# Turns of q, k, the landmarks and exp(C) by DMA from batch 3 and 2 on, scores over 64 rows, and a split first load

## The chip, the core and the metric

The kernel runs on one core of a Trainium2 chip. The core has five engines with their own instruction streams: PE (TensorE, matmuls; PEld is its weight load), DVE (VectorE), ACT (ScalarE), POOL (GpSimd) and SP (SyncE, which here only issues DMAs). PE writes to the accumulators (PSUM), the other engines read them from there; SBUF holds everything else. DMAs are issued from SP, ACT or POOL and run on 16 shared DMA engines. The metric is the device time of the program in microseconds; before the change it is 277.69 us, the median of three runs.

## What is computed

For 8 batches x 8 heads of 576 tokens with 64 features, a Nystrom attention with 32 landmarks, then a two-layer network with SiLU:

```python
q_lm = q.reshape(B, H, m, S // m, D).mean(axis=3)      # m = 32: means over 18 tokens
k_lm = k.reshape(B, H, m, S // m, D).mean(axis=3)
A  = sm(q, k_lm)        # 576 x 32 per head, sm: scaled softmax over the last axis
Bm = sm(q_lm, k_lm)     # 32 x 32
C  = sm(q_lm, k)        # 32 x 576
Z  = Bm^T / (norm_1(Bm) * norm_inf(Bm) + 1e-6)
for _ in range(6):
    Z = 2 * Z - Z @ Bm @ Z
attn = A @ Z @ C @ v
x = attn.transpose(0, 2, 1, 3).reshape(4608, 512)
h = x @ w_in            # 512 -> 2048
out = (h / (1 + exp(-h))) @ w_out                       # 2048 -> 512, float32
```

## The kernel before

**Tiling.** A batch is handled as a whole: its 8 heads are two halves (`qd` or `a`) of 4, and a head's 32 landmarks fill 32 partitions, so 4 heads x 32 landmarks make 128. q and k lie in SBUF as bf16 with partition = (head, landmark l) and in a row the 18 tokens of that landmark's segment (tiles `qn`, `kn`, two buffers each, one for even and one for odd batches).

**One batch's attention.** `landmarks` sums the 18 tokens of each segment: for batches 0 to 2 by PE with the identity as weights, from batch 3 on by a tree of additions on POOL (line 445, five for k and five for q). `turn` brings q and k into the form that PE needs, with the features on the partitions (tiles `qT`, `kT`, one buffer each): four DVE transposes of 128x576 words (lines 468 and 475); the landmarks are turned by one more (line 455, tile `lmT`). DVE turns 32x32 blocks of 4-byte words, so a word holds two features, and a score over 64 features becomes two matmuls over 32 rows (o = 0 and 1), accumulated. `scores_b`, `scores_a` and `scores_c` are those matmuls; from batch 2 on B and A go to PE as one group, C as another. A and C are written to the accumulators `h0` and `h1`. DVE transposes A's scores into `s_sb` (line 574) and takes maxima (lines 539, 590), POOL subtracts (596), ACT exponentiates: `pc` = exp(C) (line 620) and `ea` = exp(A) (line 631). `values` turns exp(C) with 12 matmuls against the identity (line 712) into `h0` and `h1`, copies it from there to `pt` (line 723: DVE; in batches 0 and 1 ACT copies one half), and multiplies by v (line 739). `steps_x` iterates Z with six small matmul and DVE steps (line 811), `z_of` closes it into `zt`.

**The network.** `mix` multiplies zt with w_in (4 heads x 2 halves, matmuls over 64 rows), through h0 and h1, into `m_sb`; `layer1` multiplies with A's weights `at` and applies SiLU (16 groups of four matmuls, alternately in h0 and h1, each with one ACT instruction of 576 columns, line 958) into `g`; `layer2` makes 128 tokens of output with 16 matmuls of 512 columns in one of two accumulators `o0`, `o1`, which ACT copies (line 989) into one of four `ost` buffers; SP issues the stores (line 1000). Two batches share a `g`, and layer 2 of a pair of batches has nine such tiles: the first four need only the even batch.

**What sets the order.** Nothing runs in program order. Every step is a node with an engine, a planned length, a priority, and the keys that it reads and writes; `_Plan.schedule` plays all engines against each other with those lengths, and the instructions are emitted in the planned order, each engine's in its own. On the chip each engine keeps that order and waits for semaphores. Steps that use the same buffer keep the order in which the program adds them: `SEQ` sets it (line 17: E is a batch's attention, S and X its first and second part, K its landmarks and turns, M the mix, L layer 1, after which the layer-2 tiles that are ready are added). `SHIFT` (line 21) moves the priorities of kinds of steps, `LOOK` is how far an engine may wait for a more urgent step, `dma_free` the planned time from which DMAs run. Layer 2 has the lowest priority on PE and fills it where nothing else is ready.

**Loads.** q, k and v of all batches and the weights are loaded by POOL, which turns float32 into bf16 on the way (lines 381, 382, 368); a load of k or q is two DMAs, one for each half of the partitions, so that heads lie in an order that `col` knows. Only batch 0's k comes from SP as float32 (`first_k`, lines 396 and 397), into space that `g` uses later, and is converted by DVE and ACT (lines 403 and 406). Batch b+2's loads are added behind batch b's attention.

Of the kernel before, what the change touches and what calls it, by code (L numbers as in the profile page):

```python
# [16 lines left out]
SEQ = ['E0', 'M0', 'S1', 'L0', 'X1', 'K2', 'M1', 'E2', 'L1', 'E3', 'M2', 'L2', 'M3', 'E4', 'L3', 'M4', 'E5', 'L4', 'E6', 'M5', 'L5', 'E7', 'M6', 'L6', 'M7', 'L7']  # L17
# [3 lines left out]
SHIFT = {'DVE gx t 3': 2.5, 'DVE qT qn 3': -0.25, 'DVE rn n 3': 0.5, 'POOL ea arec 1': 1, 'DVE amax s 3': -0.5, 'DVE lmT lm 3': 0.5, 'PE t gx 3': 2, 'DVE crec csum 3': -0.25, 'DVE asum ea 0': 2, 'POOL kn 1': -0.5, 'POOL s amax 2': 2, 'DVE s h 2': -0.5, 'DVE at ea 3': 2, 'DVE asum ea 2': 2, 'DVE kT kn 3': 1, 'ACT ea s 3': 0.5}  # L21

XM = 0.12

# [6 lines left out]
class _Plan:  # L31
# [3 lines left out]
    LOOK = 0.2  # L35
# [39 lines left out]
    def schedule(self):  # L75
# [4 lines left out]
        dma_free = 4.0  # L80
# [122 lines left out]
def kernel(  # L203
# [11 lines left out]
    LM = 32  # L215
# [32 lines left out]
    lm = [sb(f"lm{i}", [128, 2, 2, D], BF) for i in range(2)]  # L248
    lmT = [sb(f"lmT{i}", [128, 2, 2, LM, 2], BF) for i in range(2)]
# [5 lines left out]
    pc = sb("pc", [128, 2, 6, 96], BF)  # L255
# [53 lines left out]
    def emit_consts():  # L309
        V.memset(tiny, 0.0)  # L310
        V.memset(zero, 0.0)
        V.memset(mask, 0.0)
        V.memset(nmask, 0.0)
        V.memset(eps, 0.0)
        for a in range(4):
            V.memset(mask[32 * a:32 * a + 32, a, :], 1.0)
            V.memset(nmask[32 * a:32 * a + 32, a, :], -1.0)
            V.memset(eps[32 * a:32 * a + 1, :], 1e-6)
        V.memset(xp, 0.0)
        V.memset(heads_ps, 0.0)  # L320
        for a in range(4):
            V.memset(heads_ps[32 * a:32 * a + 32, a:a + 1], 1.0)
# [10 lines left out]
    def constants():  # L333
        P.add("DVE", 1.5, emit_consts, w=["mask", "xp", "zero", "tiny", "t0"], prio=-10)
# [29 lines left out]
    def load(t, src, b):  # L364
# [14 lines left out]
        def f():  # L379
            blk = rows.rearrange("(c p) n -> p c n", p=64)  # L380
            G.dma_start(out=dst[0:64], in_=blk[:, 0:4:3])
            G.dma_start(out=dst[64:128], in_=blk[:, 1:3])
        P.add("POOL", 1.4, f, w=nat_keys(t, 0) if b % 2 == 0 else [f"{t}n1"],
              dma=[1.4, 1.4], prio=-5 if b == 0 else -0.5)

    def first_k():


        st = g_sb[1].rearrange("p a n -> p (a n)").bitcast(FP)[
            :, 0:2 * SEG * D].rearrange("p (a i d) -> p a i d", a=2, d=D)  # L390
        rows = k[0].rearrange("h (l i) d -> (h l) (i d)", i=SEG).rearrange(
            "(c p) n -> p c n", p=64)
        flat = st.rearrange("p a i d -> p a (i d)")

        def f():
            nc.sync.dma_start(out=flat[0:64], in_=rows[:, 0:4:3])
            nc.sync.dma_start(out=flat[64:128], in_=rows[:, 1:3])
        P.add("SP", 1.25, f, w=["kst"], prio=-5, lat=4.0)
        for j, (i0, i1) in enumerate(((0, 7), (7, 12), (12, SEG))):
            src, dst = st[:, :, i0:i1], nat["k"][0][:, :, i0:i1]  # L400
            n = 2 * D * (i1 - i0)
            if j == 1:
                act(n, lambda src=src, dst=dst: A.copy(out=dst, in_=src),
                    r=["kst"], w=[f"kn0.{j}"], prio=-3)
            else:
                dve(n, lambda src=src, dst=dst: V.tensor_copy(out=dst, in_=src),
                    0.55, r=["kst"], w=[f"kn0.{j}"], prio=-3)
# [4 lines left out]
    def nat_keys(t, b):  # L412
        return [f"{t}n{b % 2}"] + [f"kn0.{j}" for j in range(3)] * (t == "k" and b == 0)

    def landmarks(b):
        p2 = b % 2
        for ti, t in ((1, "k"), (0, "q")):
            src = nat[t][p2]
            if b == 2:
# [3 lines left out]
            if b < 3:  # L423
                for i0 in range(0, SEG, 6):
                    def f(src=src, acc=acc, i0=i0):
# [4 lines left out]
                       w=[key], mode="full", prio=(0, 1.5, 0.5)[b], ni=12,  # L430
                       margin=0.8 * (b == 1))

                dst, src = lm[p2][:, ti], acc.rearrange("p (a d) -> p a d", d=D)
                if b == 1:
# [5 lines left out]
            else:  # L440
                tr, tk = tree, "tree"

                def add(o, a, c, n, r, w):
# [7 lines left out]
                add(lm[p2][:, ti], tr[:, :, 0], tr[:, :, 8], 128, [tk],  # L451
                    [f"lm{p2}.{ti}"])

# [9 lines left out]

    def turn(b):
        p2 = b % 2
        for qd in range(2):
# [6 lines left out]
        for qd in range(2):  # L473
# [5 lines left out]
            dve(576, f, r=[f"qn{p2}"], w=[f"qT.{qd}"], prio=3 if b else 0.9)  # L479
# [4 lines left out]
    def scores_b(b):  # L484
        lmr = lmT[b % 2]

# [12 lines left out]
        else:  # L499
            def both():  # L500
                f()
                for hf in range(2):
                    scores_a_of(b, hf)
            pe(0.6, both, r=[f"lmT{b % 2}", "qT.0", "qT.1"],
               w=["t0", "t1", "h0", "h1"], mode="32", prio=0.1, margin=0.2, ni=96)
# [16 lines left out]
    def scores_c(b):  # L522


        lmr = lmT[b % 2]
        def f():
# [9 lines left out]
        pe(0.53, f, r=[f"lmT{b % 2}", "kT.0", "kT.1"], w=["h0", "h1"], mode="32",  # L536
           prio=0.1, margin=0.2, ni=64)
# [22 lines left out]

    def scores_a(b):

        for hf, (i0, i1) in enumerate(HALF):
# [9 lines left out]
            if b > 1:  # L573
                dve(2 * n, lambda i0=i0, i1=i1, n=n, hf=hf: V.transpose(
                    out=s_sb[:, i0:i1].rearrange("p i a m -> p a i m"),
                    in_=h_ps[hf][:, :, 0:n].rearrange("p a (i m) -> p a i m", m=LM)), r=ks, w=[f"s{hf}"], prio=0.2)
# [29 lines left out]
    def exps_c(b):  # L606
# [12 lines left out]
        for qd in range(2):  # L619
            act(576, lambda qd=qd: A.activation(  # L620
                out=pc[:, qd].rearrange("p (j c) n -> p j (c n)", j=2),
                in_=h_ps[qd][:, :, 0:SH], func=AF.Exp, bias=cneg[:, qd:qd + 1],
# [4 lines left out]
    def exps_a(b):  # L627
        gate = gates(b)
        for hf, (i0, i1) in enumerate(HALF):
            n = 64 * (i1 - i0)  # L630
            act(1.3 * n, lambda i0=i0, i1=i1: A.activation(  # L631
# [493 lines left out]
```

## Time and profile before

| | us |
|---|---|
| time, three runs | 276.93, 277.69, 280.09 |
| the profiled execution: time, span from first to last instruction | 278.57, 276.9 |
| PE busy, DVE, ACT, POOL in the span | 252.8, 163.0, 165.3, 129.2 |
| layer-2 matmuls (592) busy | 142.4 |
| layer-1 matmuls (512) busy | 75.6 |
| ACT's SiLU (112 of 576 columns), mean | 0.651 |
| DVE turns of k and of q (16 each), median | 0.752, 0.755 |
| DVE copy of exp(C) turned, mean | 0.944 |
| POOL first addition of a landmark tree, mean | 2.37 |
| mean granted TensorE clock | 0.975 |

The page shows one execution. Busy times are a union over an engine's instructions; a matmul's end is modelled and overlaps the next one's start, so what a group of matmuls costs is read from starts. In a timeline each row has the start, the length, the engine, the line, the operation, output <- input, shape and how many instructions were merged; in brackets, how long the engine stood idle before it and what ended that. All matmuls have line 233, that of a helper; they are told apart by their tiles. The main groups in the page's list that touch the change:

```
L468 DVE STREAM_TRANSPOSE kT<-kn x16: 712/752/778, 13.6 to 191.3; 128x576 f32<-128x576 f32 x16
L723 DVE CAST pt<-h 96x768 bf16<-96x768 f32 x14 | 13.2, 944 | 0.0
L445 POOL TENSOR_TENSOR tree<-kn 128x1152 f32<-128x1152 bf16 x5 | 11.9, 2375 | 7.3 <-DMA kn<-in_k_dram
L596 POOL TENSOR_TENSOR s_sb<-s_sb,amax 128x512 f32<-128x512 f32 (+1 forms) x14 | 16.0, 1156 | 35.4 <-DVE amax L590
```

### The profile page before, as it was taken

How to read it: one execution, taken by the hardware profiler on the slowest of the kernel's cores; microseconds unless marked ns; L12 is line 12 of the kernel's file. 1: busy time of each engine (PE TensorE's matmuls, PEld its weight loads, DVE VectorE, ACT ScalarE, POOL GpSimd, SP SyncE). 2: the span in 40 equal slices, each digit the busy share in tenths (PEclk: the TensorE clock that was granted, in tenths of full speed). 3: DMA queues.
4: the chain of work that ended last, by engine and by line, in shares of the span. 5: the costliest groups of instructions: out<-in, count | busy, mean ns of one | idle time of the engine just before them, and what ended most of it. 6: DMA issues, size and time to landing. Idle time of an engine off the chain costs nothing.

```text
span 276.9 us, 6870 instructions
## 1 busy us (share of the span) xinstructions
PE 252.8 (91%) x2823; PEld 147.8 (53%) x2823; DVE 163.0 (59%) x388; ACT 165.3 (60%) x285; POOL 129.2 (47%) x155
## 2 busy tenths in 40 slices
PE   6178699889789999999999999999999999999994
PEld 4166475463466546645664467445755574664453
DVE  3178985997993995269936794798358822100000
ACT  2127768634686667837883688377827787761111
POOL 8234255869999999797729960321012300000000
PEclk9567999999999999999999999999999999999999
DMA  6999999999597139803593263112012210112334
GB/s 133 206 212 210 207 205 203 173 179 188 125 152 119 40 78 144 181 11 76 87 185 84 62 97 66 37 41 58 20 40 60 60 41 0 40 38 52 75 78 100
DMA packets 20288, 28.83 MB, mean 104 GB/s; under 512 B 2208, under 2 KB 11168, under 8 KB 20256
## 3 DMA queue, kind: packets, MB, share of 16 engines
q0 software_dynamic: 14048, 17.76, 39.1%
q1 hardware_dynamic: 6128, 10.56, 16.6%
q8 instruction: 22, 0.36, 0.6%
q10 hardware_dynamic: 80, 0.07, 0.1%
q14 instruction: 10, 0.08, 0.1%
HBM read 36.70 MB, written 9.44 MB: 167 GB/s over the span
## 4 chain that ended last, share of the span: by engine, by line
PE 72%; DVE 11%; DMA 6%; POOL 5%; ACT 2%; issue 2%; SPq 0%; POOLq 0%; DVEq 0%; ACTq 0%
PE o L233 39%; PE h L233 27%; PE t L233 6%; DMA g<-in_k_dram 4%; POOL tree L445 4%; DMA kn<-in_k_dram 3%; DVE pt L723 2%; DVE cmax L539 1%; DVE asum L898 1%; DVE crn L728 1%; POOL ea L907 1%; ACT g L941 1%; DVE amax L590 1%; ACT L958 0%; DVE s_sb L579 0%
## 5 line engine op out<-in xcount | busy, mean ns | idle before, releaser
L233 PE MATMUL o<-w_out_sb,g 128*128 128x512 bf16 (+1 forms) x592 | 142.4, 374 | 0.0
L233 PEld LDWEIGHTS <-g 128*128 128x128 bf16 x592 | 53.8, 98 | 52.1 <-issue 9.2
L233 PE MATMUL h<-at,m 128*128 128x288 bf16 (+2 forms) x512 | 75.6, 286 | 2.5 <-ACT m L886 1.3
L958 ACT ACTIVATE g<-h 128x576 bf16<-128x576 f32 x112 | 67.7, 651 | 14.2 <-PE h L233 14.2
L233 PEld LDWEIGHTS <-m 128*128 128x128 bf16 x512 | 49.2, 98 | 28.0 <-issue 3.8
L989 ACT COPY ost<-o 128x512 f32<-128x512 f32 (+1 forms) x37 | 21.2, 574 | 43.0 <-PE o L233 41.9
L596 POOL TENSOR_TENSOR s_sb<-s_sb,amax 128x512 f32<-128x512 f32 (+1 forms) x14 | 16.0, 1156 | 35.4 <-DVE amax L590 35.4
L840 DVE CAST m<-h 128x1024 bf16<-128x1024 f32 x14 | 17.0, 1214 | 15.7 <-PE h L233 15.7
L811 DVE SCALAR_TENSOR_TENSOR gx<-gx,t 128x384 bf16<-128x384 bf16 x30 | 16.3, 543 | 15.7 <-PE t L233 15.5
L445 POOL TENSOR_TENSOR tree<-tree 128x512 f32<-128x512 f32 (+2 forms) x30 | 24.7, 822 | 1.8
L907 POOL TENSOR_TENSOR ea<-ea,arec 128x640 bf16<-128x640 bf16 (+1 forms) x15 | 17.4, 1172 | 14.0 <-DVE arec L902 14.0
L843 ACT CAST m<-h 128x1024 bf16<-128x1024 f32 x14 | 14.2, 1012 | 14.5 <-PE h L233 14.5
L368 POOL DMA_DIRECT2D vn<-in_v_dram x24 | 14.2, 599 | 8.0 <-PE t L233 5.6
L620 ACT ACTIVATE pc<-h,cneg 128x576 bf16<-128x576 f32 x16 | 11.7, 734 | 6.5 <-DVE cneg L542 6.3
L445 POOL TENSOR_TENSOR tree<-kn 128x1152 f32<-128x1152 bf16 x5 | 11.9, 2375 | 7.3 <-DMA kn<-in_k_dram 7.2
L631 ACT ACTIVATE ea<-s_sb 128x512 bf16<-128x512 f32 (+1 forms) x16 | 13.1, 846 | 1.5 <-POOL s_sb L596 1.5
L723 DVE CAST pt<-h 96x768 bf16<-96x768 f32 x14 | 13.2, 944 | 0.0
L539 DVE TENSOR_REDUCE cmax<-h 128x1 f32<-128x576 f32 x16 | 11.4, 750 | 2.8 <-PE h L233 2.7
L233 PEld LDWEIGHTS <-ident 128*128 128x128 bf16 x108 | 8.3, 113 | 7.9 <-issue 7.8
L941 ACT ACTIVATE g<-h 128x512 bf16<-128x512 f32 (+1 forms) x16 | 9.6, 648 | 4.8 <-PE h L233 4.8
L445 POOL TENSOR_TENSOR tree<-qn 128x1152 f32<-128x1152 bf16 x5 | 11.9, 2371 | 0.4
L475 DVE STREAM_TRANSPOSE qT<-qn 128x576 f32<-128x576 f32 x16 | 11.9, 755 | 0.0
(123 smaller groups left out, 308.8 us busy)
## 6 DMA issues: line engine op xcount, KB each, us to landing
out_dram<-ost SPq DMA_DIRECT2D x70, 128.0 KB, 2.4
qn<-in_q_dram POOLq DMA_DIRECT2D x16, 288.0 KB, 8.2
vn<-in_v_dram POOLq DMA_DIRECT2D x24, 192.0 KB, 4.9
kn<-in_k_dram POOLq DMA_DIRECT2D x14, 288.0 KB, 8.4
w_out_sb<-in_moe_w_out_dram POOLq DMA_DIRECT2D x4, 512.0 KB, 16.2
w_in_sb<-in_moe_w_in_dram POOLq DMA_DIRECT2D x2, 768.0 KB, 15.8
g<-in_k_dram SPq DMA_DIRECT2D x2, 576.0 KB, 8.4
w_in_sb<-in_moe_w_in_dram POOLq DMA_DIRECT2D x2, 256.0 KB, 11.4
```

What stands on the lines that cost most here:

```text
L233: nc.tensor.matmul(out=out_ap, lhsT=lhsT, rhs=rhs, start=start, stop=stop, tile_position=tp, skip_group_check=True)
L368: G.dma_start(out=nat[t][b % 2][32 * t3:32 * t3 + 32].rearrange("p h j d -> p h (j d)"), in_=src[b].rearrange("h (l t j) d -> t l h (j d)" ...
L445: lambda: G.tensor_tensor(out=o, in0=a, in1=c, op=OP.add),
L539: dve(576, lambda qd=qd: V.tensor_reduce(out=cmax[:, qd:qd + 1], in_=h_ps[qd][:, :, 0:SH], axis=AX.XY, op=OP.max), r=[f"h{qd}"], w=[f"cmax ...
L596: E.tensor_tensor(out=sv, in0=sv, in1=mv.unsqueeze(2).to_broadcast((128, 2 * (i1 - i0), LM)), op=OP.subtract),
L723: dve(768, lambda dst=dst, src=src: V.tensor_copy(out=dst, in_=src), r=[f"h{qd}"], w=[f"pt{qd}"], prio=0.2)
L811: dve(2 * (192 - lo), lambda a=a, lo=lo, dst=dst: V.scalar_tensor_tensor(out=dst, in0=gx[a][:, :, lo:192], scalar=2.0, in1=t_ps[0][:, 0:38 ...
L840: dve(1024, lambda: V.tensor_copy(out=dst, in_=h_ps[1]), r=["h1"], w=[f"m{b % 2}.{ci}"], prio=0.1)
L843: act(1024, lambda: A.copy(out=dst, in_=h_ps[0]), r=["h0"], w=[f"m{b % 2}.{ci}"], prio=-1)
L907: lambda ev=ev, p0=p0, p1=p1, E=V if on_dve else G: E.tensor_tensor(out=ev, in0=ev, in1=arec[:, p0:p1].rearrange("p i a j -> p (i a) j").u ...
L958: act(576, lambda dc=dc, hp=hp: A.activation(out=g[:, dc, c0:c0 + S].rearrange("p (a n) -> p a n", a=2), in_=hp[:, :, 0:SH], func=AF.Silu) ...
L989: act(n, lambda ob=ob, c0=c0: A.copy(out=os_[:, c0:c0 + n], in_=ob[:, 0:n]), r=[ok], w=[sk] if c0 == 0 else [sk + "b"], prio=0.5)
```

## The change

With `TB, PB = 3, 2` two thresholds come in. From batch 3 on (`TB`):

- a load of k or q is one DMA over all 128 partitions, heads in natural order;
- the landmarks are written twice side by side (`lmd`) and turned by one DMA on SP into `lmdT`, so that the 64 features lie on partitions 0 to 63 and again on 64 to 127;
- q and k are turned by one DMA each on SP, from SBUF to SBUF, 128x128 blocks of bf16: a block holds two tokens of a segment, so even tokens' features lie on partitions 0 to 63 and odd tokens' on 64 to 127;
- the scores contract 64 features in one matmul; the two halves of the rows work on even and odd tokens;
- DVE's transpose of A's scores, ACT's exp(A) and v's index follow the new order of tokens.

From batch 2 on (`PB`) exp(C) is turned by DMA, one for each half, in place of the matmuls against the identity and the copies of `pt`; for that `pc` is 128 wide per block and cleared once.

For batch 0, POOL loads the first 12 of the 18 tokens of k's and q's segments as bf16; the last 6 come as float32, k's from SP and q's from ACT, and DVE converts them. `SEQ` has E2 before M1 and E5 before M4; `SHIFT`, `LOOK` and `dma_free` have new values, and a store's planned length on SP grows with its pieces.

```diff
-SEQ = ['E0', 'M0', 'S1', 'L0', 'X1', 'K2', 'M1', 'E2', 'L1', 'E3', 'M2', 'L2', 'M3', 'E4', 'L3', 'M4', 'E5', 'L4', 'E6', 'M5', 'L5', 'E7', 'M6', 'L6', 'M7', 'L7']
+SEQ = ['E0', 'M0', 'S1', 'L0', 'X1', 'K2', 'E2', 'M1', 'L1', 'E3', 'M2', 'L2', 'M3', 'E4', 'L3', 'E5', 'M4', 'L4', 'E6', 'M5', 'L5', 'E7', 'M6', 'L6', 'M7', 'L7']
...
+SHIFT = {'POOL ea arec 1': 1, 'DVE amax s 3': -0.5, 'PE t gx 3': 2, 'POOL kn 1': -0.5, 'DVE s h 2': -0.5, 'DVE asum ea 2': 2, 'ACT ea s 3': 0.5, 'ACT xp h 0': 2, 'PE o lmT 0': -2, 'ACT pc h 3': 1, 'DVE bt bm 2': 1, 'POOL vn 2': 0.25, 'DVE crec csum 0': 2, 'PE h m 3': -2, 'DVE amax s 2': -2, 'POOL kn 3': 1}
...
+TB, PB = 3, 2
...
-    LOOK = 0.2
+    LOOK = 0.25
...
-        dma_free = 4.0
+        dma_free = 0.0
...
+    lmd = [sb(f"lmd{i}", [128, 2, 2, 2, D], BF) for i in range(2)]
+    lmdT = [sb(f"lmdT{i}", [128, 2, 2, 128], BF) for i in range(2)]
...
-    pc = sb("pc", [128, 2, 6, 96], BF)
+    pc = sb("pc", [128, 2, 6, 128], BF)
...
+        V.memset(pc, 0.0)
...
+            if b >= TB:
+                G.dma_start(out=dst, in_=rows.rearrange("(c p) n -> p c n", p=128))
+                return
...
+            n = (SEG if b else FIRST) * D
+            G.dma_start(out=dst[0:64, :, 0:n], in_=blk[:, 0:4:3, 0:n])
+            G.dma_start(out=dst[64:128, :, 0:n], in_=blk[:, 1:3, 0:n])
...
+    FIRST = 12
+
+    def first_parts():
...
+        m = SEG - FIRST
+        for j, (t, src, q_, e) in enumerate((("k", k, nc.sync, "SP"), ("q", q, A, "ACT"))):
...
+            def f(part=part, rows=rows, q_=q_):
+                q_.dma_start(out=part[0:64], in_=rows[:, 0:4:3])
+                q_.dma_start(out=part[64:128], in_=rows[:, 1:3])
+            P.add(e, 1.3, f, w=[f"{t}st"], prio=-15, lat=4.5)
+            dve(2 * m * D, lambda t=t, part=part: V.tensor_copy(
+                out=nat[t][0][:, :, FIRST:], in_=part.rearrange(
+                    "p a (i d) -> p a i d", d=D)),
+                0.5, r=[f"{t}st"], w=[f"{t}n0.p"], prio=-3)
...
+        if b >= TB:
+            P.add("SP", 1.25, lambda: nc.sync.dma_start_transpose(
+                out=lmdT[p2].rearrange("p t a n -> p (t a) n"),
+                in_=lmd[p2].rearrange("p t a u d -> p (t a u d)")),
+                r=[f"lm{p2}.0", f"lm{p2}.1"], w=[f"lmT{p2}"], prio=-2, lat=1.8)
+            return
...
+        if b >= TB:
+            for t, dst in (("k", kTd), ("q", qTd)):
+                P.add("SP", 2.3, lambda t=t, dst=dst: nc.sync.dma_start_transpose(
+                    out=dst.rearrange("p a i n -> p (a i) n"),
+                    in_=nat[t][p2].rearrange("p a i d -> p (a i d)")),
+                    r=[f"{t}n{p2}"], w=[f"{t}T.0", f"{t}T.1"], prio=-1, lat=2.2)
+            return
...
+        def fd():
+            for qd in range(2):
+                for h in range(4):
+                    for par in range(2):
+                        r0, c0 = 64 * par, 32 * h
+                        mm(h_ps[qd][c0:c0 + 32, par, 0:SH],
+                           lmdT[b % 2][r0:r0 + 64, 0, qd, c0:c0 + 32],
+                           kTd[r0:r0 + 64, qd, :, c0:c0 + 32].rearrange(
+                               "p (t c) l -> p c t l", t=3), tp=(r0, c0))
...
+    def scores_ad(b, hf):
...
+        p0, p1 = HALF[hf][0] // 2, HALF[hf][1] // 2
+        for qd in range(2):
+            for h in range(4):
+                for par in range(2):
+                    r0, c0 = 64 * par, 32 * h
+                    mm(h_ps[hf][c0:c0 + 32, par, 0:64 * (p1 - p0)].rearrange(
+                        "p (i a l) -> p i a l", a=2, l=LM)[:, :, qd],
+                       lmdT[b % 2][r0:r0 + 64, 1, qd, c0:c0 + 32],
+                       qTd[r0:r0 + 64, qd, p0:p1, c0:c0 + 32], tp=(r0, c0))
...
         for qd in range(2):
+            if b >= PB:
+                P.add("SP", 1.25, lambda qd=qd: nc.sync.dma_start_transpose(
+                    out=pt[:, qd], in_=pc[:, qd].rearrange("p j n -> p (j n)")),
+                    r=[f"pc{qd}"], w=[f"pt{qd}"], prio=-3, lat=1.8)
+                continue
...
-                           vn[0:96, 4 * qd + h, j],
+                           vn[0:96, 4 * qd + h, j if b < TB else 2 * (j % 3) + j // 3],
...
-                    P.add("SP", 0.7, lambda store=store, i0=i0, i1=i1: store(
+                    P.add("SP", 0.64 * (i1 - i0), lambda store=store, i0=i0, i1=i1: store(
...
-    first_k()
-    load(*loads[1])
+    first_parts()
+    for x in loads[0:2]:
+        load(*x)
```

## The prediction

> **What bounds the kernel now.** I read the page's busy times and slices first, to find the stages; then the PE timeline, whose consecutive start times tell what each group of matmuls takes of a full engine; then the waits, for the stages where PE is not full; then the timeline of the first 18 us.
>
> From the page, parts 1 and 2:
>
> ```profile
> PE 252.8 (91%) x2823; PEld 147.8 (53%) x2823; DVE 163.0 (59%) x388; ACT 165.3 (60%) x285; POOL 129.2 (47%) x155
> ...
> PE   6178699889789999999999999999999999999994
> ...
> DVE  3178985997993995269936794798358822100000
> ...
> DMA  6999999999597139803593263112012210112334
> ```
>
> A slice is 6.9 us. From the thirteenth on PE stands at 9 (the last hole ends at 77.4, below), so the kernel has two parts: some 77 us with holes, in which latency counts, and some 200 us in which PE is full. A busy PE need not be a working one, so I look at the second part itself. PE's timeline over batch 3's attention (start, length, group; the lengths overlap, so a group's price is the next start less its own):
>
> ```profile
> 88.75 0.24 PE L233 MATMUL t<-lmT 32*32 32x32 bf16 x16
> 88.82 0.69 PE L233 MATMUL h<-qT,lmT 32*32 32x256 bf16 x32
> 89.44 1.90 PE L233 MATMUL o<-w_out_sb,g 128*128 128x512 bf16 x8
> 91.28 0.70 PE L233 MATMUL h<-kT,lmT 32*32 32x288 bf16 x32
> 91.91 3.63 PE L233 MATMUL o<-w_out_sb,g 128*128 128x512 bf16 x16
> 95.37 0.50 PE L233 MATMUL h<-ident,pc 128*96 128x128 bf16 x6
> 95.71 0.19 PE L233 MATMUL t<-eps,mask 128*128 128x64 bf16 x1
> ...
> 96.31 0.50 PE L233 MATMUL h<-ident,pc 128*96 128x128 bf16 x6
> 96.64 1.89 PE L233 MATMUL o<-w_out_sb,g 128*128 128x512 bf16 x8
> 98.46 0.56 PE L233 MATMUL t<-vn,pt 96*32 96x64 bf16 x48
> 98.95 0.63 PE L233 MATMUL h<-w_in_sb,zt 64*32 64x512 bf16 x16
> 99.51 0.82 PE L233 MATMUL o<-w_out_sb,g 128*128 128x512 bf16 x3
> ```
>
> Sixteen layer-2 matmuls take 91.91 to 95.37, 0.216 us each, the same as anywhere, while the softmax of batch 3 goes on at DVE and ACT. Every wait of the attention is filled with layer-2 work, so from 77 us on the time is the sum of PE's work, and a matmul taken out there is time saved, as long as nothing new keeps PE waiting.
>
> The first part, timeline of all engines:
>
> ```profile
> 1.32 0.78 POOL L381 DMA_DIRECT2D qn<-in_q_dram  x1 [0.81 <-POOLq L1109]
> ...
> 12.42 0.72 ACT L403 CAST kn<-g 128x640 bf16<-128x640 f32 x1 [10.12 <-DMA g<-in_k_dram]
> ...
> 13.11 2.08 PE L233 MATMUL t<-kn,ident 128*128 128x128 bf16 x18 [7.62 <-DVE kn L406]
> ...
> 14.99 2.12 PE L233 MATMUL t<-qn,ident 128*128 128x128 bf16 x18
> ...
> 17.45 0.31 DVE L455 STREAM_TRANSPOSE lmT<-lm 128x128 f32<-128x128 f32 x1 [1.06 <-ACT lm L438]
> ```
>
> Batch 0 waits for k until 12.42; then k's and q's landmark sums run one after the other, and nothing goes on before 17.45.
>
> **PE's work, batches 3 to 7.** The scores over 64 rows need half the matmuls per output. Batch 3's A scores move 16x256 + 16x320 = 9216 columns and take 89.44 - 88.82 = 0.62; C's 32x288 = 9216 take 91.91 - 91.28 = 0.63. The 64-row shape of the new scores is in the trace already, in the mix: 16x512 = 8192 columns take 99.51 - 98.95 = 0.56. The new A moves 16x128 + 16x160 = 4608, the new C 16x288 = 4608: 0.56 x 4608/8192 = 0.32 each. With 0.07 for B going to 0.04 a batch saves 0.30 + 0.31 + 0.03 = 0.64, five batches 3.2 us. Exp(C)'s turn leaves PE from batch 2 on: 95.71 - 95.37 and 96.64 - 96.31 are 0.67 a batch, 3.35 for batches 3 to 7 (batch 2's lies where PE has holes). Together 6.55 us.
>
> **DVE's work.** Gone are 20 turns of k and q at 0.755, five of the landmarks at 0.30, and 12 copies of pt at 0.944: 15.1 + 1.5 + 11.3 = 27.9 of 163.0 us. I cost that at nothing by itself: after 77 us PE's work covers DVE. It does free the accumulators h earlier, which the pt copies held. New on DVE are the clearing of pc (768 words per partition, about 0.8 by xp's 0.22 for 192; DVE waits for k then) and the two casts of thirds at about 0.55, ahead of k's landing. POOL issues ten loads in one piece, saving 0.6 each (6 us), and writes the landmarks double (0.46 for 128 elements, 0.73 for 256: 2.7 more); it has its lead, since batch 7's sums end at 156 and its scores start at 204.
>
> **The turns by DMA.** The trace has none. Per batch SP gets one each for k and q (590 KB), one of landmarks (131 KB), two of exp(C) (197 KB): 1.70 MB. From the page's DMA issues (KB each, us to landing):
>
> ```profile
> out_dram<-ost SPq DMA_DIRECT2D x70, 128.0 KB, 2.4
> qn<-in_q_dram POOLq DMA_DIRECT2D x16, 288.0 KB, 8.2
> ...
> w_in_sb<-in_moe_w_in_dram POOLq DMA_DIRECT2D x2, 768.0 KB, 15.8
> ```
>
> Nearest below is SP's own store, 2.4; above, the load that queues behind others, 15.8. I take 5 for k and q and 3 for the rest, nearer to the store, as it comes from the same queue and, after 90 us, meets the same thin traffic: 2x5 + 3x3 = 19 us a batch even if none overlap. The cover is the distance between scores, at 88.75, 122.8, 150.2, 174.7 and 204.0: 28.8 us on average. Batch 3's landmarks are turned at 76.65 now and used at 88.75; 3 instead of 0.3 leaves 9 us. So the turns cost nothing at 19, and at 15.8 for each of k and q (31.6 + 9 = 41) some 12 a batch.
>
> Two rules of the Trainium skill bear on this and disagree. "VectorE: DVE Perf Modes", the three transpose paths, gives 1309 ns for a 128x128 bf16 block by DMA against 390 on TensorE; a batch has 52 blocks, an estimated 68 us against the 28.8 above, by which the sum would be some 277.7 + 5 x 39 - 9.6 = 463. "Advanced Engine Details and Errata", X-Bar Transpose, says that such DMAs are as fast as plain ones. No run here shows either yet.
>
> **Waits added on SP.** A turn waits on SP for its input, and behind it queue the stores; their ost buffers (four) release ACT's copies, these the o banks, these PE. Four tiles of 16 x 0.216 are 14 us of cover. Cost 0 to 3 per batch; I take 1.5 in all, since the order on SP follows planned times that the loads can miss by a few us.
>
> **The start.** Before, k was 1.18 MB of float32 that shared the engines with q. Now SP and ACT bring 0.39 MB each at once, and POOL's first two pairs the rest: 1.57 MB written before v instead of 1.77. At the 206 to 212 GB/s of slices 2 to 4, less the slow first two us, all is written near 10.5, k near 8.5; with the 1.2 us that a landing took by the packets (k's last near 11.2), k can be used near 9.7, q near 11.7. k's sums then end at 11.7, q's at 13.6, lmT stands at 14.4 instead of 17.45: 3.0 us saved. Bounds: 0 if POOL's pieces land as k did, 4 if the clock (0.57 in 10 to 20 us) also comes up sooner. It carries on, since the loads of batches 1 and 2 have cover: PE asks for batch 2's q at 58.7, and by the DMA packets it is there near 53.
>
> **Batch 2 ahead of mix 1.** Between 71 and 77.4 PE stood idle 0.67 + 0.52 + 0.24 + 0.49 + 0.41 = 2.3 us: the spare layer-2 work had run out and layer 1 waited for batch 2's pt copies and exps. With E2 first and pt off the accumulators, mix 1 and layer 1 follow batch 2's exps, and its 0.67 of PE goes too. But mix 1 now waits for scores and exps of batch 2 (66.4 to 72.9, 6.5 us), which the 34 layer-2 matmuls left after 61 (7.3 us) just cover. I take 1.5 saved, between 3 saved and 2 lost. The new shifts and look-ahead only reorder: nothing, within that bound.
>
> **Sum.** 6.55 + 3.0 + 1.5 - 1.5 = 9.55 us. The profiled execution has a span of 276.9 and a time of 278.57, so 269.0 for it; the median of the three runs, 277.69, is 0.9 lower, so 268.1: 268.
>
> **Rivals.**
> The freed PE time is not refilled, or the start is not shortened: holes appear in the layer stages because ACT (0.651 per silu, 16 a batch) or the chain sets the pace. For it: PE waited for ACT at 77.4. Against: eight layer-1 and two layer-2 matmuls take 1.4 us where two silus take 1.3. Only 3 to 5 us would be gained: 273.
>
> SP is blocked: a turn of the next batch sits at the head of SP before its load has landed, stores pile up, PE stops. For it: batch 7's k landed 7.2 us after its issue at 138, and POOL's sums waited 5.5 for it; against, 14 us of cover. It decides once SP waits longer than the buffers last; 2 us a batch gives 278, 4 gives 288.
>
> The turns are slow: they go in rows of 128 two-byte elements, 256 B a packet. Page part 3 gives for the queues 0.12 us a packet at 1.3 to 1.7 KB (39.1% of 16 x 276.9 over 14048), and 0.055 for the smallest mean, 0.9 KB. 1.70 MB are 6660 packets; on 16 engines 23 us a batch at 0.055, 50 at 0.12. From 0.069 on they exceed the 28.8 us between scores, and the kernel waits for them: at 0.12 five batches lose 21 us each, 106 less 9.55: 374. For it: packets under 2 KB are not much cheaper than large ones. Against: nothing here shows 256 B packets. The Trainium skill's 1309 ns, quoted above, would be this case; the trace bears it out no further than that.
>
> **How the numbers follow.** One percent, 2.8 us, is about what a measurement of this kernel can tell from no change. Forecast 0.63 (268, its own range 264 to 272); not refilled 0.16 (273, still faster); SP blocked 0.13, half of it within 1% and half slower; slow turns 0.08. Faster 0.79, same 0.07, slower 0.14. Its own range runs from the start at 4, batch 2 at 3 and SP at 0 (264) to a start not shortened with 1 more lost on SP (272). The whole range goes from 263, as the lowest run lies 0.8 under the median, to 276, which takes in the first rival and leaves out slow turns and SP: 2 in 10.
>
> **What would show it.** Right: the new scores at about 0.32 from start to next start; no ident,pc group on PE after batch 1; lmT near 14.4; layer 1 of batch 1 without the hole at 75 to 77; turns landing within 3 to 6 us of issue; spare layer-2 work in every gap. Wrong: PE idle before scores or values with a DMA as releaser (slow turns), or before layer 2 with ost behind it (SP), or k still landing near 12 us.

## The result, and the profile after

The changed kernel takes 301.12 us (median of four runs, 300.65 to 301.65) against 278.89 for the kernel before beside it: a ratio of 1.0823 [1.074, 1.0906]. Times in this document are medians over all executions of a kernel, while a ratio and its interval leave out those over 1.5% slower than the kernel's fastest, so that a ratio can differ a little from the quotient of two medians; the trace of the kernel with the same order and no wait, below, is of such an execution. The forecast was 268, with a range from 263 to 276. The profiled execution took 301.28 us with a span of 299.6, 22.7 more than the span before, although PE and DVE are busy for less. Parts 1 and 2 of its page:

```profile
PE 249.0 (83%) x2595; PEld 145.3 (48%) x2630; DVE 139.9 (47%) x352; ACT 164.6 (55%) x284; POOL 128.1 (43%) x147
...
PE   5577997990299944999926999999999999999994
...
PEclk9579999998579985999985999999999999999998
DMA  7999999999992998606999359829710521111334
```

A slice is now 7.5 us. PE shows 0 and 2 in the tenth and eleventh, 4 and 4 in the fifteenth and sixteenth, 2 and 6 in the twenty-first and the next: three places at which it stands, up to 165 us, where the kernel before was full from 77. Beside and behind each the granted clock is at 5 to 8 tenths. The view of waits names one reason; the columns are the total, how often, and the longest:

```profile
PEld L236 <- DMA pt<-pc: 31.9, 8, 13.3
PE t L236 <- DMA pt<-pc: 29.8, 7, 12.8
```

PE waits for exp(C), turned by DMA (`pt<-pc`), in front of the values. PE's timeline shows two of the three places, and between them batch 3's scores, which the prediction shows for the kernel before:

```profile
80.50 0.51 PE L236 MATMUL t<-vn,pt 96*32 96x64 bf16 x24 [12.79 <-DMA pt<-pc]
81.25 0.51 PE L236 MATMUL t<-vn,pt 96*32 96x64 bf16 x24 [0.23 <-DMA pt<-pc]
81.69 1.14 PE L236 MATMUL h<-at,m 128*128 128x288 bf16 x4
82.62 0.53 PE L236 MATMUL t<-gx 128*128 128x192 bf16 x2
...
88.52 0.66 PE L236 MATMUL h<-at,m 128*128 128x288 bf16 x4
89.00 0.22 PE L236 MATMUL t<-gx 128*128 128x64 bf16 x2
...
96.16 0.21 PE L236 MATMUL t<-lmdT 64*32 64x32 bf16 x8
96.20 0.51 PE L236 MATMUL h<-qT,lmdT 64*32 64x128 bf16 x32
96.87 1.68 PE L236 MATMUL o<-w_out_sb,g 128*128 128x512 bf16 x7 [0.16 <-issue]
98.47 0.44 PE L236 MATMUL h<-kT,lmdT 64*32 64x288 bf16 x16
98.85 3.63 PE L236 MATMUL o<-w_out_sb,g 128*128 128x512 bf16 x16
...
112.53 0.51 PE L236 MATMUL t<-vn,pt 96*32 96x64 bf16 x24 [4.68 <-DMA pt<-pc]
116.74 0.51 PE L236 MATMUL t<-vn,pt 96*32 96x64 bf16 x24 [3.69 <-DMA pt<-pc]
```

Batch 2's values wait 12.79 us, batch 3's 4.68 and 3.69; batch 4's wait 3.30 at 154.76 and 4.54 at 159.81. Two layer-1 groups of the same shape show what the low clock adds: four matmuls take 82.62 - 81.69 = 0.93 us behind the first hole and 89.00 - 88.52 = 0.48 six us later.

Why the turn is late is on SP's timeline, where a row's length is the time for which the issue held SP:

```profile
58.53 9.46 SPq L500 DMA_TRANSPOSE qT<-qn  x1
68.03 1.23 SPq L1093 DMA_DIRECT2D out_dram<-ost  x2
69.43 2.75 SPq L500 DMA_TRANSPOSE kT<-kn  x1
72.28 4.07 SPq L797 DMA_TRANSPOSE pt<-pc  x2
```

Batch 2's exp(C) was written at 64.1 and 64.8. Its turns were issued at 72.28 and landed at 80.4 and 81.2: some 8 us behind batch 3's q and k on SP, and 8 us in the DMA engines. What the DMA engines did meanwhile is a count of the trace's DMA packets by their start (turns move in packets of 256 B, POOL's loads of k, q and v in packets of up to 2304 B):

```
after                turn packets   KB     load packets   KB
62 to 66 us                   293   75              261  601
66 to 74                     4315 1105               38   88
74 to 78                      124   32              190  438
78 to 80                      920  236               58  134
147 to 151 (batch 4's turn)     0    0              232  535
load held back to behind exp(C)'s turn
176 to 180                   2304  590                0    0
184 to 186                    927  237                0    0
```

With no load under way the 590 KB of a k or q turn move in under 4 us, 364 of them in the first 2. Beside a load it all but stands: 32 KB in 74 to 78. That none moves in 147 to 151 has a second reason: SP issued four stores at 144.79, just ahead of the turn and in the same queue. They are 256 packets of 2048 B, and beside the load only 100 of them start in these 4 us; the turn's first packet follows at 151.6. The load that the turn meets is one that the change itself releases at this moment: POOL's load of q for a later batch overwrites the buffer that a turn still reads, so it waits for that turn, and on SP exp(C)'s turns come next. POOL's timeline:

```profile
70.96 0.75 POOL L387 DMA_DIRECT2D qn<-in_q_dram  x1 [0.93 <-DMA qT<-qn]
...
103.39 0.73 POOL L387 DMA_DIRECT2D qn<-in_q_dram  x1 [2.15 <-DMA qT<-qn]
```

Those loads start 1.3 and 3.8 us ahead of exp(C)'s turns of batches 2 and 3 (72.28 and 107.22). From the view of DMA issues, the count and the median us from issue to landing:

```profile
pt<-pc SPq DMA_TRANSPOSE x12, 4.5
...
qT<-qn SPq DMA_TRANSPOSE x5, 6.1
kT<-kn SPq DMA_TRANSPOSE x5, 6.9
lmdT<-lmd SPq DMA_TRANSPOSE x5, 2.4
```

The start did change as meant; the timeline of all engines:

```profile
9.21 0.80 PE L236 MATMUL t<-kn,ident 128*128 128x128 bf16 x6 [4.01 <-DMA kn<-in_k_dram]
...
14.38 0.31 DVE L484 STREAM_TRANSPOSE lmT<-lm 128x128 f32<-128x128 f32 x1 [1.91 <-ACT lm L454]
14.75 0.42 PE L236 MATMUL o<-qT,lmT 32*32 32x256 bf16 x16 [0.70 <-DVE lmT L484]
```

### The profile page after: what moved, and what is told of

Read it like the earlier page. It is cut to its first block, busy times and chain, and to the rows that moved or that the text cites. A ratio compares the mean times of both kernels' runs of the same rounds, so it can differ in the third digit from the quotient of the medians.

```text
span 299.6 us, 6465 instructions
## 1 busy us (share of the span) xinstructions
PE 249.0 (83%) x2595; PEld 145.3 (48%) x2630; DVE 139.9 (47%) x352; ACT 164.6 (55%) x284; POOL 128.1 (43%) x147
## 4 chain that ended last, share of the span: by engine, by line
PE 70%; DMA 12%; DVE 6%; ACT 5%; issue 3%; SPq 2%; POOL 1%; ACTq 0%; DVEq 0%; POOLq 0%
PE o L236 37%; PE h L236 27%; DMA pt<-pc 10%; PE t L236 7%; DMA qn<-in_q_dram 2%; DVE cmax L602 1%; ACT m L936 1%; SPq L500 1%; DVE crn L821 1%; ACT ost L1082 1%; SPq L797 1%; ACT ea L720 1%; DVE s_sb L655 0%; DVE amax L672 0%; ACT L1150 0%
## 5 line engine op out<-in xcount | busy, mean ns | idle before, releaser
L236 PE MATMUL o<-w_out_sb,g 128*128 128x512 bf16 (+1 forms) x557 | 135.9, 374 | 3.4 <-issue 2.5
L236 PE MATMUL h<-at,m 128*128 128x288 bf16 (+2 forms) x512 | 79.8, 297 | 1.0 <-ACT m L979 0.5
L236 PEld LDWEIGHTS <-m 128*128 128x128 bf16 x512 | 50.8, 101 | 27.1 <-issue 3.1
L236 PE MATMUL t<-vn,pt 96*32 96x64 bf16 x288 | 4.9, 218 | 29.8 <-DMA pt<-pc 29.8
L236 PEld LDWEIGHTS <-pt 96*32 96x32 bf16 x384 | 4.4, 106 | 32.8 <-DMA pt<-pc 31.9
L845 DVE TENSOR_SCALAR gx<-t,crec,rn 128x64 bf16<-128x64 f32 x12 | 3.6, 338 | 32.6 <-PE t L236 32.6
L936 ACT CAST m<-h 128x1024 bf16<-128x1024 f32 x14 | 14.2, 1013 | 6.6 <-PE h L236 6.6
L236 PE MATMUL t<-gx 128*128 128x192 bf16 (+1 forms) x72 | 12.2, 254 | 0.0
```

Of the source, the lines that this page charges most:

```text
L236: nc.tensor.matmul(out=out_ap, lhsT=lhsT, rhs=rhs, start=start, stop=stop, tile_position=tp, skip_group_check=True)
L936: act(1024, lambda: A.copy(out=dst, in_=h_ps[0]), r=["h0"], w=[f"m{b % 2}.{ci}"], prio=-1)
```

## The experiments

The theory after this reading: exp(C)'s turns meet a load that the turns of k and q released, and PE, whose order is fixed, stands until they land. Rivals: the order on SP alone (turns of q and k ahead of exp(C)'s); the planned lengths, too short for turns; some other part of the change.

### Which part costs

Only the thresholds change: exp(C) back on PE, k, q and landmarks still by DMA:

```diff
-TB, PB = 3, 2
+TB, PB = 3, 8
```

> The changed kernel with exp(C) turned by PE again in every batch (PB = 8); q, k and landmarks still by DMA from batch 3 on, scores over 64 rows, split first load. Theory (PE stands at the values matmuls until the DMA of exp(C) has landed): of 301.1 go the 29.8 us in which PE waited for pt, and some 7 us of matmuls at half the clock behind the three long holes (13.7 us at 0.5); back come 6 x 0.67 = 4.0 us of PE: 268 to 272, and no hole over 2 us after 60 us. Rival (the turns of q and k hold PE up in their own right, as scores wait for them): holes stay, at the scores then, and the time stays above 285.

Only exp(C) by DMA:

```diff
-TB, PB = 3, 2
+TB, PB = 8, 2
```

> The changed kernel with q, k and landmarks turned by DVE again in every batch (TB = 8), exp(C) still turned by DMA from batch 2 on. If pt is late because SP issues it behind the turns of the next batch's q and k, the holes go and the time is 272 to 278. If pt is late because the loads of the next batches take the DMA engines, holes of 4 to 8 us at the values stay in batches 2 to 4 and the time is 285 to 298.

Nothing turned by DMA; what is left is the start and the order:

```diff
-TB, PB = 3, 2
+TB, PB = 8, 8
```

> The changed kernel with neither kind of turn by DMA (TB = PB = 8): what is left is the split first load, E2 before M1, E5 before M4 and the other priorities. Theory: 3 us from the start, as lmT at 14.3 instead of 17.45 shows, and up to 1.5 from batch 2: 274 to 276 against 278.9. Rival (the new order itself makes the holes, whatever turns exp(C)): 285 or more.

Measured:

| | us | ratio to before |
|---|---|---|
| exp(C) on PE, k and q by DMA | 289.43 | 1.0338 [1.028, 1.0396] |
| only exp(C) by DMA | 275.5 | 0.9838 [0.9784, 0.9892] |
| nothing by DMA | 279.62 | 1.0025 [0.9988, 1.0062] |

The first kernel misses its expectation of 268 to 272 and the third that of 274 to 276. The parts do not add. Exp(C)'s turn by itself gains 279.62 - 275.5 = 4.1 us; k's and q's by themselves lose 9.8; together they lose 21.5. So exp(C)'s turn costs 11.7 us only where k and q are turned by DMA too. The start and the new order are worth nothing measurable. That exp(C) by DMA does not hang on the new order was tried with `SEQ`, `SHIFT`, `LOOK` and `dma_free` of the kernel before (the first two as in the diff above, turned round):

```diff
-    LOOK = 0.25
+    LOOK = 0.2
...
-        dma_free = 0.0
+        dma_free = 4.0
...
-TB, PB = 3, 2
+TB, PB = 8, 2
```

> The kernel before with two parts of the change alone: the split first load and exp(C) turned by DMA from batch 2 on; order, shifts and planned numbers as before (SEQ, SHIFT, LOOK, dma_free). The run with the changed order was 275.5 (0.984). If the new order helps (batch 2 ahead of mix 1), this is slower than that, 276 to 279; if the new order costs what the start gains, as the run without any DMA turn suggests (279.6, though lmT came 3 us earlier), it is 271 to 274.

274.67 us, 0.9876 [0.9798, 0.9954]: as good as in the new order.

### The order on SP

Turns of k and q are put behind exp(C)'s on SP:

```diff
-                    r=[f"{t}n{p2}"], w=[f"{t}T.0", f"{t}T.1"], prio=-1, lat=2.2)
+                    r=[f"{t}n{p2}"], w=[f"{t}T.0", f"{t}T.1"], prio=-1, lat=2.2,
+                    after=[P.last_w["pt0"], P.last_w["pt1"]])
```

> The changed kernel, but on SP the turns of q and k of a batch are planned behind the turns of exp(C) of the batch before. If SP's order is the cause, all three holes go: 270 to 276. If it is only a part (the first hole, where exp(C) stood ready at 64.9 and was issued at 72.3; the other two were issued 3 and 2 us after exp(C) was ready), one hole shrinks by some 7 us and its slow clock goes: 288 to 296.

302.48 us, 1.0784 [1.0703, 1.0866]: no better, and outside both ranges expected. Yet the wait for exp(C) is gone (1.9 us in all); others have come in its place. Lines of PE's timeline with the long holes:

```profile
99.98 1.87 PE L236 MATMUL o<-w_out_sb,g 128*128 128x512 bf16 x4 [7.29 <-ACT ost L1083]
...
145.90 1.11 PE L236 MATMUL h<-at,m 128*128 128x288 bf16 x4 [11.25 <-ACT pc L703]
...
169.34 0.68 PE L236 MATMUL h<-qT,lmdT 64*32 64x128 bf16 x32 [5.55 <-DMA qT<-qn]
```

The largest names exp(C) on ACT (`pc`), and its cause lies two engines away. POOL's timeline:

```profile
113.21 1.28 POOL L461 TENSOR_TENSOR tree<-tree 128x512 f32<-128x512 f32 x1
127.36 0.73 POOL L387 DMA_DIRECT2D qn<-in_q_dram  x1 [12.87 <-DMA qT<-qn]
...
141.96 2.27 POOL L679 TENSOR_TENSOR s_sb<-s_sb,amax 128x512 f32<-128x512 f32 x2
```

POOL issues in order. A load that waits 12.87 us for q's turn holds the landmark sums behind it, these hold the subtraction of A's maximum (line 679), for which ACT waits 10.62 us, and exp(C) of the batch comes behind that on ACT. So q's and k's turns may come neither ahead of exp(C)'s nor late: a load on POOL hangs on them. With exp(C) on PE the same chain shows once (a hole of 5.94 us at 163.33 behind exp(C), with ACT 6.58 behind line 678), so the 9.8 us there are of this kind at least in part.

### The meeting with the load

Now the load itself is held back: a POOL step of 0.2 us reads `pt` before the loads of k and q of batch b+2, so they start only when exp(C)'s turns have landed.

```diff
+    gate_t = sb("gate_t", [128, 2, 2], BF)
...
-              w=nat_keys(t, 0) if b in (2, 4, 6) else [f"{t}n0"] if b == 0 else [f"{t}n1"],
+              r=["gate"] if b >= PB + 2 else [], w=nat_keys(t, 0) if b in (2, 4, 6) else [f"{t}n0"] if b == 0 else [f"{t}n1"],
...
+            if b >= PB and b + 2 < B:
+                P.add("POOL", 0.1, lambda: G.tensor_tensor(
+                    out=gate_t, in0=pt[:, :, 5, 96:98], in1=pt[:, :, 5, 96:98], op=OP.add),
+                    r=["pt0", "pt1"], w=["gate"])
```

> The changed kernel, with one small POOL addition that reads the turned exp(C) of batch b before the loads of k and q of batch b+2 (b from 2 on); nothing else differs. If the turns of exp(C) are slow because these loads take the DMA engines, they land within 3 to 4 us in every batch (median 4.5, longest 10.5 before; 2.8 where k and q were turned by DVE). The time need not fall: POOL itself now waits, and what is queued behind on it (maxima subtracted, weights) comes later: 285 to 302.

> The same kernel as the run with loads behind exp(C)'s turns (one look gave 279.2), now timed. Theory (the whole loss against before is the meeting of these loads with the turns of exp(C)): 277 to 281, that is 0.99 to 1.01 of before, although every DMA turn stays where it was. Rival (that look was a lucky one): 290 or more.

A first execution took 279.22 us, below the 285 to 302 expected; ten more have the median 278.98, 1.0025 [0.9982, 1.0069]: 22.1 us of the loss are gone, although every turn by DMA is still there. By the packet count no load moves between the issue of exp(C)'s turns and the first values in any batch (in the changed kernel 590, 548 and 569 KB in batches 2 to 4). From its DMA issues:

```profile
pt<-pc SPq DMA_TRANSPOSE x12, 2.8
...
kT<-kn SPq DMA_TRANSPOSE x5, 4.7
```

and from its waits:

```profile
POOL tree L462 <- DMA kn<-in_k_dram: 13.8, 5, 4.7
POOL gate_t L1176 <- DMA pt<-pc: 11.4, 4, 4.1
...
PE t L236 <- DMA pt<-pc: 6.4, 7, 1.6
PE o L236 <- ACT ost L1083: 2.5, 2, 1.6
```

PE's wait for exp(C) falls by 29.8 - 6.4 = 23.4; the spans differ by 299.6 - 276.4 = 23.2.

But a step more on POOL also alters the planned order. So the next kernel has the same order on every engine, and only the wait differs: the step reads `pc`, which is written earlier, in place of `pt`.

```diff
-                    out=gate_t, in0=pt[:, :, 5, 96:98], in1=pt[:, :, 5, 96:98], op=OP.add),
+                    out=gate_t, in0=pc[:, :, 5, 94:96], in1=pc[:, :, 5, 94:96], op=OP.add),
```

> Instruction for instruction the kernel of load_behind_pt, in the same order on every engine, but its small POOL addition reads exp(C) itself instead of the turned exp(C): the loads of k and q no longer wait for the turn to land, only for its input. Theory (the loads that run beside the turns of exp(C) are the loss): the turns land late again, 4 to 10 us, PE waits over 15 us for them, 285 to 300. Rival (POOL's other order, not the wait, made load_behind_pt fast): within 2 us of 279.

295.98 us, 1.0589 [1.0501, 1.0678]. The traces of the two have the same order on every engine. The wait alone is worth 295.98 - 278.98 = 17.0 us by the medians, and 1.0589 - 1.0025 of some 278.8, 15.7 us, by the ratios to the kernel before beside each. Its trace, of the execution that took 303.44 us, has:

```profile
PE t L236 <- DMA pt<-pc: 25.6, 8, 7.9
```

The meeting is back: in batch 5 loads issued at 175.92 and 176.67 move 1168 KB between the turns' issue at 177.42 and the values at 185.56. The other 5 to 6 us of the 22.1 fall, by difference, to the changed order.

All 13 traces with exp(C) turned by DMA say the same together. Of their 156 such turns 155 have a landing on record. The 123 beside which no load moves, from issue to landing, land after 2.7 to 4.7 us, at the median 2.8; the 21 with more than 540 KB of load beside them take 5.3 to 12.1, at the median 9.4. The 11 with 25 to 334 KB lie between, at 2.8 to 4.3.

### The planned lengths

The plan had a turn land 2.2 us (k, q) or 1.8 us (exp(C)) after its issue. With longer ones the order could mend itself:

```diff
-                P.add("SP", 2.3, lambda t=t, dst=dst: nc.sync.dma_start_transpose(
+                P.add("SP", 2.75, lambda t=t, dst=dst: nc.sync.dma_start_transpose(
...
-                    r=[f"{t}n{p2}"], w=[f"{t}T.0", f"{t}T.1"], prio=-1, lat=2.2)
+                    r=[f"{t}n{p2}"], w=[f"{t}T.0", f"{t}T.1"], prio=-1, lat=4.0)
...
-                    r=[f"pc{qd}"], w=[f"pt{qd}"], prio=-3, lat=1.8)
+                    r=[f"pc{qd}"], w=[f"pt{qd}"], prio=-3, lat=7.0)
```

> The changed kernel with other planned lengths only: a turn of k or q 2.75 us on SP and 4.0 to land (2.3 and 2.2 before), one of exp(C) 7.0 to land (1.8). The same instructions on the same engines, in an order that expects late turns. Theory (fixed orders on PE and POOL that wait for turns planned too short are the whole loss): the waits of PE for pt fall from 29.8 us to under 8 and the time is 270 to 282. Rival (the turns' DMA traffic as such costs the time, in whatever order): 290 or more.

With 8.0 in place of 4.0 for k and q:

> As the one before, with 8.0 us for a turn of k or q to land, so that POOL's loads into the buffers that these turns read are planned later and POOL should not stand before them (it stood 12.9 us for one such load where the turns of exp(C) came first). If POOL's wait is what is left after the longer plan, this gains a further 3 to 8 us; if not, within 2 us of it.

300.68 us, 1.0847 [1.0719, 1.0975], and 295.17, 1.0584 [1.0448, 1.072]. The longest lengths recover some 6 us of the 22, the shorter ones nothing: planned lengths alone are not the main cause. They move the order, and not the load that a turn releases. Both times lie where the rival of the first expectation has them, that the turns' traffic costs the time in whatever order; but with the held load all that traffic stays and the time is 278.98, so that rival falls.

### What the turns of k and q are worth without the meeting

Three more kernels have the held load. In the order of before, with k, q and exp(C) by DMA (`TB, PB = 3, 2`), and with exp(C) alone (`TB, PB = 8, 2`):

> The loads behind exp(C)'s turns, and order, shifts and planned numbers as before the change (SEQ, SHIFT, LOOK, dma_free); all DMA turns and the scores over 64 rows stay. With exp(C) alone turned by DMA the old order was worth 275.5 - 274.7 = 0.8 us. If that holds here, 276 to 280; if the new order was made for late turns and the old one was not, 282 or more.

> q, k and landmarks turned by DVE (TB = 8), exp(C) by DMA, split first load, order as before, and the loads of k and q behind exp(C)'s turns. Without the last part 274.7. There the turns of exp(C) landed in 2.8 us anyway, as the loads did not start with them, so the gate has nothing to mend: 274 to 277, and 277 if POOL's added waits (12.7 us in the run with all DMA turns) cost anything.

277.64 us, 0.9988 [0.9952, 1.0025], and 278.69, 0.9963 [0.9918, 1.0007]. They can't be told apart, so turning k and q by DMA, with scores over 64 rows, brings nothing measurable even with the meeting removed. Holding the load may have a price of its own: without it the second of them takes 274.67, 4.0 us less by the medians and some 2.4 by the ratios (0.9963 and 0.9876), but the intervals overlap, so it is not shown. With the held load in the new order and turns planned longer (2.75 on SP, 6.0 to landing):

> The loads behind exp(C)'s turns, and the turns of k and q planned at 2.75 us on SP and 6.0 to land. With no load in their way they land 4.7 to 6.3 us after issue; a plan that knows it should keep POOL from standing before loads whose buffer a turn still reads: 272 to 278. If POOL's place is not what is left: 278 to 282.

282.11 us, 1.0079 [1.0024, 1.0135]: no gain over the short lengths. By the medians it is 3.1 slower, but the intervals of the ratios overlap.

The last kernel asks whether a load beside exp(C)'s turn costs as much when no turn of k or q stands on SP: exp(C) alone by DMA, k and q on DVE, and the loads released by `pc`, early.

```diff
-TB, PB = 3, 2
+TB, PB = 8, 2
...
+                P.add("POOL", 0.1, lambda: G.tensor_tensor(
+                    out=gate_t, in0=pc[:, :, 5, 94:96], in1=pc[:, :, 5, 94:96], op=OP.add),
+                    r=["pc0", "pc1"], w=["gate"], prio=-4)
```

> The other way round: q, k and landmarks turned by DVE (that kernel took 275.5, its turns of exp(C) landed in 2.8 us), and the loads of k and q of batch b+2 made to start when exp(C) of batch b is ready, that is with its turns. Theory (the meeting alone is enough): the turns take 4 to 10 us and PE waits for them, 280 to 292. Rival (it takes the turns of q and k on SP as well): 274 to 277.

272.93 us, 0.9786 [0.9705, 0.9867]. The question stays open, since the meeting did not come about: POOL issued the loads 2.5 to 3.2 us after the first of the two turns, and the turns of batches 2 to 5 landed in 2.8 as they do alone. A small meeting is in the traces of the other two kernels with k and q on DVE and no held load: in batch 2, 42 to 334 KB of load move beside exp(C)'s turns, which land after 3.2 to 4.3 us. But it is the fastest of all, 28.2 us below the change and 6 below the kernel before. Why it is 2.6 us faster than exp(C) by DMA without that step was not separated; its order differs too, and the intervals overlap.

## Why the prediction was wrong, step by step

**Turns at nothing (the step that failed).** "The cover is the distance between scores", 28.8 us, was the right cover for k and q and landmarks. Exp(C)'s turn lies elsewhere: between ACT's exp and the values on PE, which in PE's fixed order come a few us later. That cover is just enough for a turn alone: with k and q on DVE and landings of 2.8 us at the median, PE's waits for exp(C) are 1.5 us in all, and in the old order none. With the held load the same median leaves 6.4 us of waits, and landings of 5 us and more leave the holes. The prediction added all five turns to 19 us a batch and set them against a cover that only three of them have.

**Thin traffic (its second half).** The 5 and 3 us a turn were near what a turn takes without the meeting (at the median 4.7 for k, 6.2 for q and 2.8 for exp(C) with the held load), and the prediction took the traffic for thin after 90 us. But the change turns batch 3's q and k and batch 2's exp(C) at 58 to 76 us, where the DMA line that the prediction shows has 9, 9 and 5 tenths (slices 9 to 11), and there lies the longest hole. Above all it had no term for the load that a turn releases. This is what made 2.8 into 4.5 at the median and up to 10.5, and PE's wait into 29.8; that the load's start costs 16 to 17 us is shown by the pair of kernels in one order.

**Waits on SP.** Its 1.5 us and the rival of 278 to 288 had stores pile up behind a blocked turn. The turn at 58.53 did hold SP for 9.46 us; but what was late behind it was exp(C)'s turn. In batch 4 exp(C)'s turn itself stood behind four stores. Nor is SP's order the cause to be mended: with exp(C) ahead, the loads on POOL took the place of the wait at the same total. The prediction listed who waits behind a turn on SP, and not who waits behind POOL's load that waits for the turn.

**Slow turns.** This rival (0.055 to 0.12 us a packet) fell: a packet of 256 B takes 0.018 us at the median. The trace of the kernel before could have told: its SP packets take 0.074 us at 1024 B and 0.347 at 4608 B, so small packets are cheaper nearly in proportion, where the prediction, with "not much cheaper than large ones", went by the means of whole queues. The Trainium skill's figure of 1309 ns for a 128x128 block ("VectorE: DVE Perf Modes", the three transpose paths) is not borne out as a cost per block of a large turn: k's 18 blocks landed in 4.7 us. The other rule that the prediction quotes, of the Trainium skill's "Advanced Engine Details and Errata", X-Bar Transpose, agrees in so far as a turn alone moved 364 KB in 2 us, 182 a us, and the changed kernel's turns 288 KB from 68.5 to 69.5, where the fullest slices of loads have 204 to 218 a us; beside a load it does not hold.

**PE's work.** Exp(C)'s 0.67 a batch is borne out: 3.35 us forecast, 4.1 found by itself, DVE's copies and batch 2 included. The scores were mis-sized: B and A go from 0.69 to 96.87 - 96.16 - 0.16 = 0.55, C from 0.63 to 0.38, so 0.39 a batch and not 0.64. The price by columns of a 512-column shape did not carry over to matmuls of 128 to 288 columns.

**DVE's work.** 27.9 us off and some 2 on were forecast; the page has 163.0 - 139.9 = 23.1 less. That it is worth nothing by itself was right: k's and q's turns moved off DVE gained nothing.

**The start.** lmT's first use was forecast near 14.4 and came at 14.75; with the earlier sums PE was ahead by an estimated 5 us of work at 60 us (each matmul up to then at its price in the kernel before; the kernel with nothing by DMA against the kernel before). That it "carries on" was wrong: by the same estimate the lead is some 3 at 80, 1 to 2 at 150 and none at 190. From 60 to 80 its granted clock is 0.91 against 1.00 before, and the layers wait for `gx`, a step of Z's iteration; where the rest goes stays open.

**Batch 2 ahead of mix 1.** 1.5 us forecast, nothing found: the two orders are within 0.8 us of each other with exp(C) by DMA.

**The sum.** 9.55 us forecast; what was found by parts is 4.1 for exp(C), 0 for start and order, and no gain for k and q, so 4.1 and not 9.55 without the meeting, and a loss of 22 with it. Besides the start's lead one thing stays open: a third pair of buffers for k and q would part the load from the turn; it wasn't tried.

## What to carry to other kernels

A DMA that reads a buffer is also the release of the next load into it: cost it together with the transfer that it sets free, with whatever small, urgent transfer is issued just behind, and with what stands ahead of that one in its queue. Set a moved step's time against the distance to its own consumer in the fixed order, not against that of the largest gap nearby, and follow every in-order queue that waits for it, the one that issues the next load too. A wait in front of the load, or a turn that stays on an idle engine, can be worth more than the engine time that the turn saves.

## What the runs showed of the hardware

Beside a load a turn by DMA nearly stops. In 62 to 66 us 293 turn packets of 256 B went beside 261 load packets of 2304 B, in 76 to 78 it was 112 beside 112: about one for one, so near a ninth of the bytes. The Trainium skill says that an engine takes turns between its queues, a whole packet at a time ("DMA: Bandwidth & Descriptors", Queues, rings and completion order). Those counts agree if the packets of the trace are the packets of that rule, which no run here shows. Within SP's queue the order of issue held: in 147 to 151 us the 232 load packets had 100 packets of stores beside them, and the turn issued behind these stores had none until 151.6.

An issue of one k or q turn holds SP for 2.4 to 3.8 us in the changed kernel, and once for 9.46; 1363 KB of loads moved between that issue and its landing.

A hole costs more than its length. The windows view of the changed kernel, with the window, its length, busy time and count of PE, PEld, DVE, ACT and POOL, then the granted clock, the DMA share and GB/s:

```profile
76.00:80.50 4.50, 0.00 (x1) 0.00 (x1) 0.00 (x0) 0.00 (x0) 0.00 (x0) 0.50 1.19 172
80.50:83.90 3.40, 3.17 (x59) 2.14 (x59) 1.90 (x5) 0.65 (x1) 1.82 (x4) 0.50 0.54 162
83.90:86.20 2.30, 2.30 (x12) 1.62 (x11) 1.01 (x2) 1.30 (x2) 2.21 (x3) 0.50 1.19 173
86.20:95.00 8.80, 8.68 (x65) 6.05 (x66) 1.79 (x5) 6.71 (x12) 8.17 (x9) 1.00 0.65 104
```

The clock stays at half for 5.7 us after PE has resumed at 80.5, for 3.5 after 116.7 (to 120.2) and for 4.8 after 159.8 (to 164.6). From 72.56 to 164.71 the trace's stretches of one clock are 13.65, 23.89, 10.24, 34.13 and 10.24 us long, each a whole multiple of 3.413 to within 0.01, as if the clock were set at such steps only. PE was busy for some 14.2 us at half clock there, which at full clock would be an estimated 7 less. The Trainium skill puts the return to full clock at about 3.4 us of sustained work ("TensorE: Matmul & The Clock Gate", Part 1: The HAM clock gate); the 3.5 agrees, the other two were longer.
